# Layer statistics and a flag sent through DRAM instead of TensorE, with sums copied by ScalarE and a rewritten schedule

## The chip, the core and the metric

One NeuronCore of a Trainium2 chip runs the kernel. The metric is the device time of one execution in microseconds (us), taken as the median of several runs. The engines are TensorE (PE in the profile; PEld is its weight load), VectorE (DVE), ScalarE (ACT), GpSimd (POOL) and SyncE (SP). SP only issues transfers here; GpSimd issues those that add to what lies at their destination.

## The reference

The input `x` has 2048 rows of 640 numbers. It is normalized row by row, and the result is the sum of the input, a state-space convolution with a skip term, and a two-layer network with Mish between the layers.

```python
xn = (x - mean(x)) / sqrt(var(x) + 1e-5)            # over the 640 columns
# A: K[d, l] = 2 Re(sum_n C[d, n] exp(A[d, n] dt[d] l));  y = causal convolution of xn with K
a = y + xn * D_skip
# B: w1 is 640 x 1728, w2 is 1728 x 640
h = xn @ w1 + b1
b = (h * tanh(softplus(h))) @ w2
return x + a + b
```

## The kernel before

The rows are cut into four blocks of 512 (`NB`), which the kernel holds transposed: 640 columns as five groups (`KD`) of 128 partitions, 512 rows along the free axis. The 1728 hidden columns are 14 tiles (`NF`), all of 128 but one of 64. Every float32 operand of a product is split into two float16 parts, hi and lo, and a product is made of three matmuls (hi hi, lo hi, hi lo).

For each block and each hidden tile, TensorE makes the first product (`mm1`, L807), ScalarE and VectorE work out Mish in eight steps (L890 to L926), and TensorE adds the tile's second product (`mm2`, L859) to five sums `ACC`, one bank of PSUM each. The second product of a tile comes three tiles after its first (`LAG`). In blocks 1 to 3 twelve of the tiles go in six pairs (`PAIRS`): sums of weights and sums of input quarters replace part of the products (L827), which takes small copies and additions between product groups: `cV`, `cY` on ScalarE (L1049, L1050), `z`, `w` on VectorE (L1053, L1057).

Beside this run:
- the normalization of the next block c. SP loads its rows (L1106), VectorE takes mean and variance (L627 to L629), GpSimd makes `st_row`, 128 partitions by 2 x 4 numbers: four means and four reciprocal deviations (L633, L634, L1213). TensorE transposes them into 8 rows of 128 (`spread`, L638), in the bank `TR` that the pairs also use; ScalarE copies them out of PSUM (`sr`, L642); SP writes them to DRAM (`sd`, L646) and reads them back spread over all 128 partitions, means and deviations (`bc`, L650). VectorE then subtracts and multiplies in each of the five groups of the transposed block `XT` (L654, 2 x 5 steps), after which come the hi and lo parts (L565, L568) and the differences for the pairs (L613 to L620);
- the convolution as two running sums over time with three coefficients per column (`skip_a` to `skip_e`, L743 to L763), which is what it is for small steps and rates. Whether the inputs allow that, and the scaling of the split, is checked on the chip: VectorE leaves one number in each partition (`ok`, L728), a matmul with a matrix of ones adds them over the partitions (`ok_sum`, L731), VectorE compares with 127.5 (L737) and each engine reads the flag (`load_flag`, L734). If it is set, a general version runs behind;
- the output of a finished block: the sums leave PSUM (`join`: k = 0 and 1 on VectorE, L768; 2 to 4 on ScalarE, L770), GpSimd adds the input by an accumulating transfer (L548), adds that to `XT` by another (L773) and stores it (L776). The last block is drained by VectorE and SP (L933, L934).

The first block's normalization and first products, up to 20 us, are a hand-written list (`ORDER`). Behind it the order is a plan made when the program is built (`Plan`): each step has a cost, predecessors, a buffer to take or drop, and for transfers a size. TensorE's steps are in the order in which they are added. From these and the costs each other step gets a due time, worked backwards, and each engine takes the ready step that is due first. The plan sets only the order; on the chip semaphores hold each step until its inputs are there.

Of the kernel before, what the change touches and what calls it, by code (L numbers as in the profile page):

```python
# [20 lines left out]
P = 128  # L21
# [37 lines left out]

class Plan:  # L60


    GAP = {"PE": 0.22, "ACT": 0.12, "DVE": 0.12, "SP": 0.0, "POOL": 0.3}
# [74 lines left out]
    def run(self):  # L138
        self.dues()
        todo = {e: {} for e in self.t}  # L140
# [312 lines left out]
def body(ctx: ExitStack, tc: tile.TileContext, x, xT, logA, Aim, Cr, Ci, logdt, vec, w1, w1T, w2, w2T, out):  # L453
# [29 lines left out]
    ones = cst.tile([P, P], F32, name="ones")  # L483
    g.memset(ones, 1.0)
# [42 lines left out]
    pl.pool("b", [[row.tile([P, TB], F32, name=f"bc{j}") for j in range(2)]])  # L527
# [108 lines left out]
    def spread():  # L636

        pe.transpose(TR[:2 * NT, 0:P], NX["st"].rearrange("p j i -> p (j i)"), ident)  # L638

    def spread_a():  # L640
        NX["sr"] = tmp.tile([2 * NT, P], F32, name="sr")
        a.copy(NX["sr"], TR[:2 * NT, 0:P])  # L642

    def spread_d():
        NX["sd"] = dram.tile([2 * NT, P], F32, name="sd")
        sp.dma_start(NX["sd"], NX["sr"])  # L646

    def spread_l(c):
        for j in range(2):
            sp.dma_start(pl["b", c][j], NX["sd"][j * NT:(j + 1) * NT].rearrange("(o i) p -> o (i p)", o=1).to_broadcast([P, TB]))  # L650

    def norm_t(c, k, j):
        z = XT[c][:, k]
        v.tensor_tensor(z, z, pl["b", c][j], op=(OP.subtract, OP.mult)[j])  # L654
# [9 lines left out]
    def mode_ops():  # L664
# [6 lines left out]
        yield "ACT", 3.4, lambda: a.activation(t()[:, 0], t()[:, 0], AF.Exp)  # L671
# [3 lines left out]
        for k in range(KD):  # L675
            yield "ACT", 0.5, lambda k=k: a.activation(t()[:, 2, k], t()[:, 2, k], AF.Copy, accum_out=sm[:, 0, k:k + 1])
# [53 lines left out]
    def ok_sum():  # L730
        pe.matmul(TR[:, 0:1], ones, SM["ok"], start=True, stop=True)  # L731
# [4 lines left out]
    def ok_end():  # L736
        v.tensor_scalar(flag, TR[0:1, 0:1], P - 0.5, None, op0=OP.is_lt)  # L737
# [27 lines left out]
    def join(b, k):  # L765
        r = pl["r", b, k]
        if k < 2:
            v.tensor_scalar(r, ACC[k], 1 / SO, None, op0=OP.mult)  # L768
        else:
            a.activation(r, ACC[k], AF.Copy, scale=1 / SO)  # L770
# [165 lines left out]
    def whole():  # L936
# [9 lines left out]
        def chain(b, f, pre, drop=()):  # L946
# [3 lines left out]
            if b > 0 and f in PAIRS:  # L950
                add(("sX", *n), A, 0.36, sig, b, f, PX, CA, pre=[("two", *n)], take=("s", ("s", *n), 2))
                add(("vX", *n), V, 0.38, mul, b, f, PX, CA, pre=[("sX", *n)], take=("A", ("A", *n), 1))
                add(("sg", *n), A, 0.36, sig, b, f, PZ, CB, pre=[("three_b", *n), ("sX", *n)])
                add(("v1", *n), V, 0.38, mul, b, f, PZ, CB, pre=[("sg", *n), ("vX", *n)], drop=[("s", *n)])
            else:
                add(("sg", *n), A, t(0.60, 0.36), sig, b, f, pre=pre, take=("s", ("s", *n), 2))
                add(("v1", *n), V, t(0.68, 0.38), mul, b, f, pre=[("sg", *n)], take=("A", ("A", *n), 1), drop=[("s", *n)])
            add(("a1", *n), A, t(0.63, 0.36), mish_a1, b, f, pre=[("sg", *n)], take=("p", ("p", *n), 1), drop=[("s", *n)])
            add(("a2", *n), A, t(0.63, 0.36), mish_a2, b, f, pre=[("a1", *n)])
            add(("a3", *n), A, t(0.63, 0.36), mish_a3, b, f, pre=[("a2", *n)])  # L960
            add(("v3", *n), V, t(0.61, 0.36), mish_v3, b, f, pre=[("a3", *n), ("v1", *n)], drop=[("p", *n)])
            add(("a4", *n), A, t(0.54, 1.44), mish_a4, b, f, pre=[("v3", *n)], take=("h", ("h", *n), 1))
# [40 lines left out]
        for f in range(3, NF):  # L1003
# [4 lines left out]
            if f == 7:  # L1008
                add(("spread", 1), M, 0.1, spread, pre=[("rs", 1)])
# [338 lines left out]
```

## Time and profile before

| | |
|---|---|
| median of 3 runs | 357.88 us (357.68 to 357.89) |
| span of the profiled execution, first to last instruction | 356.0 us |
| granted TensorE clock, mean | 1.000 |
| instructions | 6197 |
| traffic of the transfers | 48.75 MB |

In the profile a group is named by line, engine, operation and `out<-in`, with its count, its busy time and the mean duration of one instruction in ns. Durations overlap a little: an instruction is fed while the one before it finishes, so a step of 0.72 us is followed by the next after 0.61. The chain of waits is followed back from the last instruction; each of its pieces has a start, a length and what ran. In the timeline the columns are start, duration, engine, line and operation, and in brackets the idle time before it and what ended that. A POOL or SP transfer there is its issue, not its movement; the page's last part has the time from issue to landing.

### The profile page before, as it was taken

Reading aid. Unit: us, or ns where it says so; the run is one execution under the profiler, and the core shown is the slowest. Engines: PE = TensorE matmul, PEld = TensorE weight load, DVE = VectorE, ACT = ScalarE, POOL = GpSimd, SP = SyncE. Lnnn points to the kernel's source line nnn. Section 1 sums busy time; section 2 is a strip of 40 time slices with the busy share of each in tenths; the row PEclk is TensorE's granted clock in tenths of the full one; section 3 lists DMA queues with packets and bytes.
Section 4 is the critical chain, followed back from the end, with each engine's and each line's share of the span. In section 5 each row is a group of like instructions: output and inputs, shape, how many; then the busy total and the mean of one; then the engine's idle time right before and its main releaser. Section 6 shows DMA issues by size and latency. Waiting matters only on the chain.

```text
span 356.0 us, 6197 instructions
## 1 busy us (share of the span) xinstructions
PE 350.0 (98%) x2257; PEld 215.1 (60%) x2257; DVE 305.9 (86%) x583; ACT 295.8 (83%) x620; POOL 48.9 (14%) x74
## 2 busy tenths in 40 slices
PE   7999999999999999999999999999999999999996
PEld 6754444444666666665566666566566666666543
DVE  5989989989999999999999877899988878895552
ACT  4699999987598699989899977989989979877650
POOL 2200010000014221000004341000002443000000
PEclk9999999999999999999999999999999999999999
DMA  7869964402819926910445982931000994032004
GB/s 266 327 175 288 321 217 121 142 0 66 287 56 159 295 71 142 347 40 3 130 151 88 252 204 77 309 120 40 28 0 7 164 216 102 18 58 32 2 2 152
DMA packets 26052, 48.75 MB, mean 137 GB/s; under 512 B 3592, under 2 KB 6944, under 8 KB 26016
## 3 DMA queue, kind: packets, MB, share of 16 engines
q1 hardware_dynamic: 19488, 34.86, 30.0%
q0 software_dynamic: 6240, 13.11, 18.5%
q8 instruction: 19, 0.31, 0.4%
q10 hardware_dynamic: 288, 0.33, 0.3%
q14 instruction: 17, 0.14, 0.2%
HBM read 39.10 MB, written 5.26 MB: 125 GB/s over the span
## 4 chain that ended last, share of the span: by engine, by line
PE 96%; DVE 1%; DMA 1%; ACT 0%; issue 0%
PE acc L859 48%; PE h L827 18%; PE h L807 12%; PE tr L827 12%; PE h L800 2%; PE h L789 2%; PE tr L789 1%; DMA x<-in_A_u_dram 1%; PE acc L1236 0%; DVE st L627 0%; DVE st L628 0%; ACT x L1224 0%; PE acc L873 0%; PE acc L871 0%; PE acc L870 0%; DVE w1l L556 0%
## 5 line engine op out<-in xcount | busy, mean ns | idle before, releaser
L859 PE MATMUL acc<-hi,w2h 128*128 128x512 f16 x273 | 100.9, 379 | 0.0
L859 PE MATMUL acc<-hi,w2l 128*128 128x512 f16 (+1 forms) x265 | 99.7, 379 | 0.0
L859 PE MATMUL acc<-lo,w2h 128*128 128x512 f16 x253 | 93.3, 379 | 0.0
L859 PEld LDWEIGHTS <-w2h 128*128 128x128 f16 x526 | 50.9, 98 | 48.3 <-issue 2.1
L890 ACT ACTIVATE s<-h,cv 128x512 f32<-128x512 f32 (+1 forms) x55 | 32.7, 595 | 28.6 <-PE h L827 23.4
L827 PEld LDWEIGHTS <-w1h 128*128 128x128 f16 x432 | 42.3, 98 | 10.7
L910 DVE SCALAR_TENSOR_TENSOR A<-p,A 128x512 f32<-128x512 f32 (+1 forms) x56 | 37.1, 662 | 8.5 <-ACT p L906 8.2
L859 PEld LDWEIGHTS <-w2l 128*128 128x128 f16 x273 | 25.6, 98 | 30.7 <-issue 1.1
L926 DVE SCALAR_TENSOR_TENSOR lo<-A,hi 128x512 f16<-128x512 f32 x52 | 35.5, 683 | 8.0 <-ACT hi L916 8.0
L894 DVE SCALAR_TENSOR_TENSOR A<-h,bs,s 128x512 f32<-128x512 f32 (+1 forms) x55 | 34.9, 637 | 6.2 <-ACT s L890 6.2
L898 ACT ACTIVATE p<-s,kc 128x512 f32<-128x512 f32 (+1 forms) x56 | 39.4, 703 | 0.6
L902 ACT ACTIVATE p<-p,kc 128x512 f32<-128x512 f32 (+1 forms) x56 | 39.4, 703 | 0.5
L906 ACT ACTIVATE p<-p,kc 128x512 f32<-128x512 f32 (+1 forms) x56 | 39.3, 702 | 0.4
L916 ACT ACTIVATE hi<-A 128x512 f16<-128x512 f32 x52 | 32.5, 626 | 2.6 <-DVE A L910 2.5
L548 POOL DMA_DIRECT2D r<-in_xT_dram x15 | 13.4, 1003 | 131.7 <-DVE r L768 66.3
L749 DVE TENSOR_TENSOR_SCAN g<-g,car,kc 128x512 f32<-128x512 f32 x20 | 25.6, 1278 | 1.7 <-ACT g L743 1.7
L827 PEld LDWEIGHTS <-w1l 128*128 128x128 f16 x216 | 21.1, 98 | 8.2
L753 DVE TENSOR_TENSOR_SCAN g<-g,car,g 128x512 f32<-128x512 f32 x20 | 25.5, 1276 | 0.0
L827 PE MATMUL tr<-xh,w1l 128*128 128x256 f16 x90 | 24.5, 273 | 0.0
L827 PE MATMUL tr<-xh,w1h 128*128 128x256 f16 x90 | 24.5, 273 | 0.0
L827 PE MATMUL tr<-xl,w1h 128*128 128x256 f16 x90 | 24.5, 273 | 0.0
L827 PEld LDWEIGHTS <-swh 128*128 128x128 f16 x216 | 21.1, 98 | 4.4
(177 smaller groups left out, 726.6 us busy)
## 6 DMA issues: line engine op xcount, KB each, us to landing
w<-in_w_dram SPq DMA_DIRECT2D x25, 320.0 KB, 4.9
x<-in_A_u_dram SPq DMA_DIRECT2D x14, 320.0 KB, 5.0
w<-in_w2T_dram SPq DMA_DIRECT2D x15, 288.0 KB, 6.4
w<-in_B_w_dram SPq DMA_DIRECT2D x13, 320.0 KB, 3.4
w<-in_w1T_dram SPq DMA_DIRECT2D x13, 320.0 KB, 7.0
xt<-in_xT_dram SPq DMA_DIRECT2D x15, 256.0 KB, 5.6
r<-in_xT_dram POOLq DMA_DIRECT2D x15, 256.0 KB, 5.6
xt<-r POOLq DMA_DIRECT2D x15, 256.0 KB, 4.6
```

The costliest lines, as they stand in the source:

```text
L749: v.tensor_tensor_scan(g1[:, 1:], g1[:, 1:], zero.to_broadcast([P, TB]), car[:, 1, k:k + 1], op0=OP.add, op1=OP.add)
L807: pe.matmul(o, w, x, start=(j == 0), stop=(j == len(order) - 1))
L827: pe.matmul(o, p, q, start=start and n == 1, stop=n == 3 * len(w), skip_group_check=True)
L859: pe.matmul(o, w, x, start=start, stop=stop)
L890: a.activation(pl["s", b, f][:, c], bank(b, f)[:, c] if h is None else h, AF.Sigmoid, bias=cv[:, f:f + 1], scale=1 / SH)
L894: v.scalar_tensor_tensor(pl["A", b, f][:, c], bank(b, f)[:, c] if h is None else h, bs[:, f:f + 1], pl["s", b, f][:, c], op0=OP.add, op1=O ...
L898: a.activation(pl["p", b, f][:, cols(f)], pl["s", b, f][:, cols(f)], AF.Arctan, bias=one, scale=-1.0)
L902: a.activation(p, p, AF.Square, bias=pi4, scale=2.0)
L906: a.activation(p, p, AF.Tanh, bias=mb, scale=MG)
L910: v.scalar_tensor_tensor(A, pl["p", b, f][:, cols(f)], MC, A, op0=OP.add, op1=OP.mult)
L916: a.activation(hi, A, AF.Copy, scale=MA * SA / SH)
L926: v.scalar_tensor_tensor(lo, A, MA * SA / SH, hi, op0=OP.mult, op1=OP.subtract)
```

## The change

- The transposes `spread`, the copies `spread_a` and the matmul `ok_sum` go, with the matrix `ones`. The statistics are written to DRAM from `st_row` as GpSimd leaves it, element by element in transposed order: 8 x 128 numbers of 4 bytes.
- GpSimd stores the mean with its sign changed. Only the deviations are spread into `bc` (one row buffer in place of two). The means are added to `XT` by five accumulating transfers per block, issued by GpSimd, whose source is the row in DRAM repeated for 128 partitions; VectorE is left with the multiplication.
- The `ok` numbers go to DRAM and back as one row of 128; VectorE takes their minimum and compares it with 0.5.
- ScalarE makes all five copies of the sums of a block.
- In the plan, the costs of most steps and two of the gaps are changed, the orders that follow from `spread`, `sr` and `ok_sum` go, and a table `SHIFT` moves the due times of 139 numbered steps by -30 to +30 us.

```diff
+SHIFT = [e.split(":") for e in (
+    "5:16 27:12 30:-15 33:19 36:-20 51:-17.5 55:7.5 61:5 67:-4.5 72:-6.5 79:4 83:-9.5 84:-6.5 90:-16 97:-30 105:7.5 "
...
-    GAP = {"PE": 0.22, "ACT": 0.12, "DVE": 0.12, "SP": 0.0, "POOL": 0.3}
+    GAP = {"PE": 0.17, "ACT": 0.14, "DVE": 0.12, "SP": 0.0, "POOL": 0.3}
...
+        ops = list(self.ops.values())
+        for i, x in SHIFT:
+            for u in ("due", "soft"):
+                ops[int(i)][u] += float(x)
...
-    pl.pool("b", [[row.tile([P, TB], F32, name=f"bc{j}") for j in range(2)]])
+    pl.pool("b", tiles(row, "bc", 1, [P, TB]))
...
-    def spread():
-        pe.transpose(TR[:2 * NT, 0:P], NX["st"].rearrange("p j i -> p (j i)"), ident)
-    def spread_a():
-        NX["sr"] = tmp.tile([2 * NT, P], F32, name="sr")
-        a.copy(NX["sr"], TR[:2 * NT, 0:P])
     def spread_d():
         NX["sd"] = dram.tile([2 * NT, P], F32, name="sd")
-        sp.dma_start(NX["sd"], NX["sr"])
+        sp.dma_start(NX["sd"].rearrange("r p -> p r"), NX["st"].rearrange("p j i -> p (j i)"))
     def spread_l(c):
-        for j in range(2):
-            sp.dma_start(pl["b", c][j], NX["sd"][j * NT:(j + 1) * NT].rearrange("(o i) p -> o (i p)", o=1).to_broadcast([P, TB]))
-    def norm_t(c, k, j):
+        sp.dma_start(pl["b", c], NX["sd"][NT:2 * NT].rearrange("(o i) p -> o (i p)", o=1).to_broadcast([P, TB]))
+    def center(c, k):
+        g.dma_start(XT[c][:, k], NX["sd"][0:NT].rearrange("(o i) p -> o (i p)", o=1).to_broadcast([P, TB]), accum_op=OP.add)
+    def norm_t(c, k):
         z = XT[c][:, k]
-        v.tensor_tensor(z, z, pl["b", c][j], op=(OP.subtract, OP.mult)[j])
+        v.tensor_tensor(z, z, pl["b", c], op=OP.mult)
...
-    def ok_sum():
-        pe.matmul(TR[:, 0:1], ones, SM["ok"], start=True, stop=True)
+    def ok_row():
+        NX["ok"] = tmp.tile([1, P], F32, name="ok_row")
+        z = dram.tile([P], F32, name="ok_dram", bufs=1)
+        sp.dma_start(z.rearrange("(p o) -> p o", o=1), SM["ok"])
+        NX["okd"] = z
+    def ok_back():
+        sp.dma_start(NX["ok"], NX["okd"].rearrange("(o p) -> o p", o=1))
     def ok_end():
-        v.tensor_scalar(flag, TR[0:1, 0:1], P - 0.5, None, op0=OP.is_lt)
+        z = tmp.tile([1, 1], F32, name="ok_all")
+        yield lambda: v.tensor_reduce(z, NX["ok"], axis=AX.X, op=OP.min)
+        yield lambda: v.tensor_scalar(flag, z, 0.5, None, op0=OP.is_lt)
...
     def join(b, k):
         r = pl["r", b, k]
-        if k < 2:
-            v.tensor_scalar(r, ACC[k], 1 / SO, None, op0=OP.mult)
-        else:
-            a.activation(r, ACC[k], AF.Copy, scale=1 / SO)
+        a.activation(r, ACC[k], AF.Copy, scale=1 / SO)
...
-                add(("cV", *n), A, 0.36, lambda: a.copy(PVS, PV), pre=[("one", *n)] + ([] if first else [("w", *p0)]))
-                add(("cY", *n), A, 0.36, lambda: a.copy(PY, PX), pre=[("cV", *n), lastC])
+                add(("cV", *n), A, 0.27, lambda: a.copy(PVS, PV), pre=[("one", *n)] + ([] if first else [("w", *p0)]))
+                add(("cY", *n), A, 0.304, lambda: a.copy(PY, PX), pre=[("cV", *n), lastC])
...
-            add(("sr", c), A, 0.25, spread_a, pre=[("spread", c)])
-            add(("sd", c), S, 0.1, spread_d, pre=[("sr", c)], kb=4.0)
+            add(("sd", c), S, 0.1, spread_d, pre=[("rs", c)], kb=200.0)
...
-                add(("n", c, k, 0), V, 0.62, norm_t, c, k, 0, pre=[("lxt", c), ("bc", c)], drop=[("b", c)])
-                add(("n", c, k, 1), V, 0.62, norm_t, c, k, 1, pre=[("n", c, k, 0)], drop=[("b", c)])
+                add(("n", c, k, 0), G, 1.0, center, c, k, pre=[("lxt", c), ("sd", c)], kb=512.0)
+                add(("n", c, k, 1), V, 0.602, norm_t, c, k, pre=[("n", c, k, 0), ("bc", c)], drop=[("b", c)])
...
+        add(("okd",), S, 0.1, ok_row, pre=last, kb=1.0)
+        add(("okr",), S, 0.1, ok_back, pre=[("okd",)], kb=1.0)
+        fns = list(ok_end())
+        add(("oke", 0), V, 0.2, fns[0], pre=[("okr",)])
+        add(("oke",), V, 0.17, fns[1], pre=[("oke", 0)])
...
-        g.tensor_copy(NX["st"][:, 0], NX["mv"][:, :, 0])
+        g.tensor_scalar(NX["st"][:, 0], NX["mv"][:, :, 0], -1.0, None, op0=OP.mult)
```

More of the change, by code (lines that the diff above doesn't have):

```diff
@@ L958, in chain @@
[L958 to L962, printed above, removed]
@@ L1138, in whole @@
             for j in range(4):
[L1139 removed]
+                add(("ss", i, j), V, 0.336, sum_w, i, j, pre=both + ([("ss", i - 1, 3)] if i and j == 0 else []) + ([("ss", i, 0)] if j == 1 else [("ss", i, 1), ("ss", i, 2)] if j == 3 else []),
                     take=("t", ("ss", i, j // 2), 3 if j == 0 else 1) if j in (0, 2) else None, drop=drops[j])
```

84 lines of the change are left out of this document (38 added, 46 removed), and 9 rows, old and new, of the table SHIFT.

## The prediction

> **What bounds the kernel now.** I read the page first (busy time of each engine, the forty slices, the chain that ended last), then the waits of TensorE, then the chain of waits piece by piece, and last the stretches in which the changed operations run.
>
> ```profile
> PE 350.0 (98%) x2257; PEld 215.1 (60%) x2257; DVE 305.9 (86%) x583; ACT 295.8 (83%) x620; POOL 48.9 (14%) x74
> PEclk9999999999999999999999999999999999999999
> PE 96%; DVE 1%; DMA 1%; ACT 0%; issue 0%
> PE tr L1246 <- POOL ident masks.py:199: 1.5, 1, 1.5
> PE acc L1236 <- ACT x L1224: 1.0, 1, 1.0
> ```
>
> The first three lines are the page's: TensorE (PE) is busy 98%, its granted clock is full in all slices, and it carries 96% of the chain. Busy time alone wouldn't settle it, since modelled matmul ends overlap the gaps. The last two lines are all that the view of TensorE's waits holds, and both belong to the opening (L1246 fills time with idle products, L1236 transposes the first input). So I followed the chain, whose columns are start, length and what ran:
>
> ```profile
> 9.18 0.34 DVE xl L1242
> ...
> 20.34 3.24 PE h L807 x15
> ...
> 46.24 3.24 PE h L807 x15
> 49.48 0.11 PE tr L638
> 49.58 3.24 PE acc L859 x15
> ...
> 134.91 0.11 PE tr L638
> ...
> 219.51 0.11 PE tr L638
> ...
> 321.59 0.12 PE tr L731 x2
> 321.71 1.32 PE acc L859 x6
> ...
> 324.01 1.29 PE acc L859 x6
> ...
> 352.60 0.02 issue
> ```
>
> Each piece begins where the one before it ends. 15 matmuls of 512 columns take 3.24 us in the early and the late pieces, 0.216 us each, and no piece between 20.34 and 352.60 belongs to another engine. For 332 us TensorE waits for nothing. Whatever frees VectorE, ScalarE or a queue in that stretch saves nothing; the program gets shorter only by TensorE instructions that go away, or at its two ends.
>
> **What goes from TensorE.** Three transposes of the statistics (L638) and the flag's matmul (L731, in two passes). On the chain they are 0.11 + 0.11 + 0.11 + 0.12 = 0.45 us, and the six products behind L731 take 1.32 in place of 1.29, so 0.48 us in all. Nothing hides them: the pieces on either side touch. When they go the next matmul group moves up, if what it needs is there.
>
> **The ends.** At the start the chain runs over the load of the input, VectorE and ScalarE until 9.5, where TensorE's piece begins; the hand-written opening is kept, and the memset of `ones` that goes lies on GpSimd (POOL) outside this chain. At the end the last store and its drain stay. I take zero for both, with bounds of plus and minus 0.3 us: the order of everything else moves, so a shift of the size of the opening's last VectorE step (0.34 us, the first row of the fence above) can't be excluded either way.
>
> **VectorE and ScalarE.**
>
> ```profile
> L654 DVE TENSOR_TENSOR xt<-xt,bc 128x512 f32<-128x512 f32 x30 | 20.0, 683 | 0.0
> L768 DVE TENSOR_SCALAR r<-acc 128x512 f32<-128x512 f32 x6 | 4.0, 683 | 0.0
> L770 ACT ACTIVATE r<-acc 128x512 f32<-128x512 f32 x9 | 5.2, 594 | 1.2 <-PE acc L859 0.8
> L642 ACT COPY sr<-tr 8x128 f32<-8x128 f32 x3 | 0.7, 238 | 0.0
> 226.00:262.00 36.00, 36.00 (x232) 22.18 (x231) 34.20 (x57) 33.14 (x73) 0.00 (x0) 1.00 0.30 104
> ```
>
> The 15 subtractions leave VectorE (half of the first row, 15 x 0.683 = 10.2 us), and so do the six copies of sums (4.1 us): 14.3 of 305.9. ScalarE takes those copies over, 6 x 0.594 = 3.6 us, and loses the three copies of `sr`, 0.7: it gains 2.9. On the path to the end both count zero. The relief is real where it falls: in the last row, the stretch ahead of the fourth block, VectorE is busy 34.2 of 36.0 us, and five subtractions, 3.4 us, leave it.
>
> The copies have a deadline. At a block boundary the five sums must be copied out before TensorE writes the next block's first products over them:
>
> ```profile
> 188.28 0.68 DVE L768 TENSOR_SCALAR r<-acc 128x512 f32<-128x512 f32 x1
> 189.78 0.68 DVE L768 TENSOR_SCALAR r<-acc 128x512 f32<-128x512 f32 x1
> 192.00 0.38 PE L859 MATMUL acc<-hi,w2h 128*128 128x512 f16 x1
> ```
>
> The second copy ends at 189.78 + 0.68 = 190.46, TensorE needs the first bank at 192.00: over 1.5 us to spare. From 188.28 to 192.00 ScalarE has 3.7 us for two copies of 0.594 that it did not have; 2.5 are left for the Mish steps and sigmoids, which are wanted three tiles later. It fits if the planner puts the copies first. I take zero; the upper bound is one lost copy pair, 1.2 us, at each of three boundaries.
>
> **The statistics.** Today they wait for a place on TensorE and in its bank; after the change the rows go to DRAM as GpSimd leaves them. The third time is the tightest:
>
> ```profile
> 212.11 0.18 POOL L1213 COPY st_row<-mv 128x4 f32<-128x4 f32 x1
> 220.06 0.91 POOL L773 DMA_DIRECT2D xt<-r  x1 [5.96 <-DVE xt L763]
> 224.02 0.56 POOL L776 DMA_DIRECT2D out_dram<-xt  x1 [3.04 <-DMA xt<-r]
> 231.46 1.29 DVE L654 TENSOR_TENSOR xt<-xt,bc 128x512 f32<-128x512 f32 x2
> 258.21 1.31 PE tr L827 x12
> SPq L650 <- DMA sd<-sr: 4.3, 3, 3.0
> xt<-r POOLq DMA_DIRECT2D x15, 256.0 KB, 4.6
> r<-in_xT_dram POOLq DMA_DIRECT2D x15, 256.0 KB, 5.6
> L548 POOL DMA_DIRECT2D r<-in_xT_dram x15 | 13.4, 1003 | 131.7 <-DVE r L768 66.3
> q1 hardware_dynamic: 19488, 34.86, 30.0%
> ```
>
> The rows are ready at 212.3. The small write of them was waited for up to 3.0 us on SP's queue; the new one has 1,024 elements of 4 bytes. Below, I price it like the old one. Above: the last row gives 0.30 x 16 x 356 / 19488 = 0.088 us a packet of some 2 KB, and if each element cost as much, 64 on each of 16 engines add 5.6 us. So it lands between 215.3 and 220.9. Then GpSimd issues five accumulating transfers, at 1.003 us each, which land 4.6 to 5.6 us after issue: the last one at 225 to 231.5. VectorE began its subtractions at 231.46 today and no longer does them. So even the slow end is in time and the step costs zero; I take the fast end, being nearest the row of the same write. The first two blocks' statistics come in the same order. GpSimd's added issue time is 15 x 1.003 = 15.0 us on an engine that is 14% busy; behind it in its queue stand the output's accumulations and stores, none of which TensorE waits for soon. On SP the row broadcast halves (three transfers fewer), and what stands behind its wait are weight-check loads.
>
> A rule of the Trainium skill speaks against this write: "DMA: Bandwidth & Descriptors", Rules for kernel authors, says that a strided last dimension becomes one descriptor per element and should be rearranged to be contiguous. By that page's 10.5 ns a packet (section Bandwidth), 64 per engine would be an estimated 0.7 us; no run here shows a 4-byte write of data. By it the sum would stay as it is.
>
> **The flag.**
>
> ```profile
> L728 DVE TENSOR_TENSOR ok<-ok,z x1: 153/153/153, 314.2 to 314.2; 128x1 f32<-128x1 f32 x1
> L734 PEldq TENSOR_LOAD <-flag x1: 487/487/487, 330.7 to 330.7; - x1
> ```
>
> From 314.4 it now takes two transfers, up to 3.0 us each by the row above, and two small VectorE steps of 0.15: ready near 320.7, and TensorE reads it at 330.7, ten microseconds later. Cost zero; without that cover, up to 6 us.
>
> **The sum.** 356.0 - 0.48 = 355.5 us of span. The runs' median is 357.88, 1.9 above the profiled span (launch and end, outside it; I keep it): **357.4 us**, 0.13% less. A measurement of this kernel can tell about 0.2%, 0.7 us, from no change, so the likeliest answer is "within".
>
> **Due times and planned costs.** They reorder ScalarE, VectorE, SP and GpSimd; TensorE's own order is written out and stays. As TensorE waits for none of them now, there is no wait to remove, so the gain is zero; what it may cost is the first rival.
>
> **The rivals.**
> - *New due times misplace ScalarE's copies inside the pairs (slower).* Each pair's second product group waits for two short copies:
>
> ```profile
> 157.41 0.37 ACT L1049 COPY pvs<-tr 128x256 f32<-128x256 f32 x1 [0.52 <-PE tr L827]
> 157.68 0.38 ACT L1050 COPY h<-tr 128x256 f32<-128x256 f32 x1
> 158.67 0.98 PE tr L827 x9
> ```
>
>  The copies end at 158.06, TensorE goes on at 158.67: 0.6 us, the tightest place that I found. Against it: today's order keeps it everywhere. For it: the planned costs of ScalarE's steps are cut, so the plan holds less reserve, and over a hundred due times move by up to 30 us. It decides once two steps of about 0.6 us stand ahead of the copies: 0.6 us of stall. At three such pairs, one in each later block, 1.8: 359.2 us. Chance 0.12.
> - *The five copies at the boundaries come too late (slower).* From the point where more than 2.5 us of other ScalarE work goes ahead; up to 1.2 us at three boundaries: 361.0, half of it 359.2. Chance 0.06.
> - *The accumulating transfers queue on GpSimd behind two stores that wait for their data (slower).* Each store costs the wait for the accumulation before it, 4.6 to land and 0.9 of issue: 11 us behind 225 to 231.5, so VectorE would begin at 236 to 242.5 in place of 231.46, with 3.4 us less to do, and end its preparation 1 to 8 us later than today. It decides once that exceeds the lead that the preparation has on the products at 258.21; with half of it passed on once, 4.5 us, 361.9. Chance 0.05.
> - *The gain is eaten by short waits (no change).* The 0.48 us come back as tenths in 18 pairs: 357.5 to 358.5. Nothing in the trace shows such waits now. Chance 0.17.
> - *Faster by over 0.2%.* It needs another 0.24 us beyond all of TensorE's removed work, from the ends; 357.1 with my 0.3. Chance 0.08.
>
> **How the numbers follow.** The forecast has 0.52, with no change 0.69 within; slower 0.12 + 0.06 + 0.05 = 0.23; faster 0.08. The range runs from 357.0 (0.48 and the 0.3 at the ends, rounded) to 359.4, which holds the pairs' and half of the boundaries' case; left out are the queue's case, worse stalls and little below, about 0.15.
>
> **What would show it.** Right: no L638 or L731 pieces, a chain of touching TensorE pieces from 20.3 to about 352.1, no new line in the waits of TensorE, 15 multiplications and no copy of sums on VectorE. Wrong: a wait of TensorE on ScalarE's copies inside a pair (first rival), on sums at 107, 192 or 276 (second), on hi/lo parts of the input near 174 or 258 (third), or a TensorE piece that begins before 9.5.

## The result and the profile after

The changed kernel takes **381.78 us** (median of five runs, 380.98 to 385.35), the kernel before 357.89 beside it. The ratio is 1.069, 95% interval 1.0657 to 1.0726: 23.9 us slower. The profiled execution of it took 385.35 us, with a span of 382.3. Where some executions of a run came out over 1.5% slower than its others (two of x3's four, one of x4's four), the time given is the median of the others.

The page of the changed kernel (TensorE's busy time, its granted clock in forty slices, the chain that ended last):

```profile
PE 357.0 (93%) x2252; PEld 216.9 (57%) x2252; DVE 294.6 (77%) x563; ACT 296.9 (78%) x623; POOL 62.5 (16%) x88
PEclk9999999999999999959999999989999999999999
PE 53%; DMA 21%; DVE 16%; ACT 5%; issue 3%; POOL 1%; SPq 0%; POOLq 0%
```

TensorE has five instructions less (2252 in place of 2257) and VectorE's busy time is 11.3 us shorter; 14.3 were foreseen. But TensorE is busy for 93% of the span in place of 98%, transfers (DMA) now carry 21% of the chain, and in one slice the granted clock is half. The span is 26.3 us longer: TensorE is idle 25.3 us in place of 6.0, and busy 7.0 us longer with five instructions less. Pieces of the chain, with start, length and what ran:

```profile
147.93 8.61 DMA w<-in_w1T_dram
156.58 7.71 DMA xt<-sd
164.31 0.69 DVE xt L666
...
166.57 4.00 PE h L844 x18
...
222.77 8.72 DMA sd<-st_row
231.55 3.90 DMA bc<-sd
235.71 8.27 DMA xt<-sd
244.00 0.69 DVE xt L666
...
337.86 6.74 DMA ok_dram<-ok
344.65 3.24 DMA ok_row<-ok_dram
```

Where the chain of before was TensorE without a gap, it is now, at the three places shown, transfers, then VectorE, then TensorE. (It leaves TensorE between 35 and 111 us as well, but there TensorE itself waited little, 5.3 us in the 100 from 40 on.) In order: a load of weights and an accumulating transfer that takes off a mean; the statistics' small write, the broadcast and another accumulating transfer; the flag's write and read. The load of weights and the broadcast stand in the chain because the profile names what landed last; nothing in the code makes an accumulating transfer wait for either. In both cases an older transfer of GpSimd's own landed at the same moment (at 156.3 the first accumulating one of the block, at 235.4 one of the output's), and that is the likelier releaser. VectorE at the first of these places, as its timeline shows (start, length, line, operation; in brackets its idle time before it and what ended that):

```profile
149.24 0.68 DVE L927 SCALAR_TENSOR_TENSOR A<-p,A 128x512 f32<-128x512 f32 x1
156.29 0.69 DVE L666 TENSOR_TENSOR xt<-xt,bc 128x512 f32<-128x512 f32 x1 [6.37 <-DMA xt<-sd]
158.49 0.69 DVE L666 TENSOR_TENSOR xt<-xt,bc 128x512 f32<-128x512 f32 x1 [1.51 <-DMA xt<-sd]
164.31 0.69 DVE L666 TENSOR_TENSOR xt<-xt,bc 128x512 f32<-128x512 f32 x1 [1.96 <-DMA xt<-sd]
166.11 0.41 DVE L1064 TENSOR_TENSOR h<-h,pvs 128x256 f32<-128x256 f32 x1
```

The multiplications (L666) prepare the next block's input, but they stand at the head of VectorE's queue, and VectorE takes its instructions in order. Behind them stands the sum L1064 of the block under way, which TensorE needs at once. TensorE's waits have such entries in place of none:

```profile
PE tr L844 <- ACT h L1061: 4.7, 3, 2.6
PE acc L876 <- DVE lo L943: 3.8, 3, 3.0
PE h L844 <- DVE h L1064: 3.5, 1, 3.5
PE h L817 <- DVE A L911: 2.7, 1, 2.7
```

(Total, times, longest, in us.) Why the transfers are late shows in two views. GpSimd's timeline at block 1:

```profile
48.16 0.65 POOL L1223 TENSOR_SCALAR st_row<-mv 128x4 f32<-128x4 f32 x1
59.77 2.92 POOL L662 DMA_DIRECT2D xt<-sd  x3 [10.96 <-DMA sd<-st_row]
68.81 0.90 POOL L662 DMA_DIRECT2D xt<-sd  x1 [6.12 <-issue]
70.99 0.88 POOL L662 DMA_DIRECT2D xt<-sd  x1 [1.27 <-issue]
```

The rows are ready at 48.8, the small write lands 11 us later, three accumulating transfers are issued, and the fourth only when the first has landed. And the stretches of time (start and end, length, busy time and count for PE, PEld, DVE, ACT and POOL, granted clock, DMA share, GB/s), the first two at block 1's statistics, the third at block 2's, the others at block 3's:

```profile
49.50:59.30 9.80, 9.37 (x65) 4.80 (x64) 9.62 (x21) 9.77 (x21) 0.00 (x0) 1.00 0.79 30
59.50:64.00 4.50, 4.50 (x23) 2.06 (x21) 2.06 (x6) 2.27 (x6) 2.92 (x3) 1.00 0.89 276
138.20:146.50 8.30, 8.30 (x69) 5.53 (x69) 8.09 (x16) 7.83 (x17) 0.51 (x1) 1.00 0.14 32
223.20:231.30 8.10, 8.10 (x59) 5.52 (x58) 6.25 (x9) 5.84 (x14) 2.20 (x4) 1.00 0.68 82
231.50:240.00 8.50, 7.92 (x53) 5.08 (x52) 5.26 (x9) 5.94 (x16) 3.59 (x5) 1.00 0.98 267
```

While block 1's small write is under way the DMA engines count as 79% busy and move 30 GB/s; as soon as it has landed, 276. There the write of 4 KB is not only slow, what is issued behind it comes late as well. Four weight loads stood on SP's queue just behind it. The view of the changed kernel's load line L561, for those issued from 49.3 to 51.3, closes with their time from issue to landing:

```profile
DMA to landing us min/median/max: 12.4/12.8/13.1
```

The same view of the kernel before, of the three such loads (L543) issued from 48.7 to 51.3:

```profile
DMA to landing us min/median/max: 3.2/3.3/3.4
```

Outside SP's queue too: the output store that GpSimd issued at 222.70 landed at 231.50, in the moment in which the small write issued at 222.77 did. Block 2, where TensorE loses most, is another case: no load was issued behind the small write (the DMA share is 0.14), because SP, which takes its instructions in order too, stood at the broadcast's read until the write had landed (its wait 7.9 us), 8.4 us after the write's issue. Six weight loads and the first three accumulating transfers then started within 6 us of one another.

### The profile page after: what moved, and what is told of

Same layout as the page of the kernel before. It is cut to its first block, busy times and chain, and to the rows that moved or that the text cites. A ratio compares the mean times of both kernels' runs of the same rounds, so it can differ in the third digit from the quotient of the medians.

```text
span 382.3 us, 6201 instructions
## 1 busy us (share of the span) xinstructions
PE 357.0 (93%) x2252; PEld 216.9 (57%) x2252; DVE 294.6 (77%) x563; ACT 296.9 (78%) x623; POOL 62.5 (16%) x88
## 4 chain that ended last, share of the span: by engine, by line
PE 53%; DMA 21%; DVE 16%; ACT 5%; issue 3%; POOL 1%; SPq 0%; POOLq 0%
PE acc L876 25%; PE h L844 13%; PE tr L844 7%; DMA w<-in_B_w_dram 7%; DMA xt<-sd 6%; PE h L824 3%; DMA sd<-st_row 2%; DMA w<-in_w1T_dram 2%; DVE A L911 2%; DMA ok_dram<-ok 2%; PE h L806 2%; DVE g L773 1%; DVE lo L943 1%; DVE A L927 1%; ACT s L907 1%
## 5 line engine op out<-in xcount | busy, mean ns | idle before, releaser
L876 PE MATMUL acc<-lo,w2h 128*128 128x512 f16 x253 | 94.3, 383 | 3.8 <-DVE lo L943 3.8
L844 PEld LDWEIGHTS <-w1l 128*128 128x128 f16 x216 | 21.2, 98 | 15.6 <-issue 7.9
```

Source lines behind the costliest of these rows:

```text
L844: pe.matmul(o, p, q, start=start and n == 1, stop=n == 3 * len(w), skip_group_check=True)
L876: pe.matmul(o, w, x, start=start, stop=stop)
```

## The experiments

The theory that I took into the first runs, "late statistics": the small write and the accumulating transfers land far later than the order of the work assumes, and VectorE's multiplications wait for them with TensorE's work behind. The rivals: "copies and flag" (ScalarE's copies or the flag's two transfers), and "due times" (the table `SHIFT` orders the work badly). The recorded expectations call the accumulating transfer that takes off a mean a center, and the copies of the sums joins.

**One part at a time (four runs).** *x1*, the kernel before with ScalarE's copies and the flag through DRAM:

```diff
-        pe.matmul(TR[:, 0:1], ones, SM["ok"], start=True, stop=True)
...
+        sp.dma_start(z.rearrange("(p o) -> p o", o=1), SM["ok"])
...
+        sp.dma_start(NX["ok"], NX["okd"].rearrange("(o p) -> o p", o=1))
...
-        v.tensor_scalar(flag, TR[0:1, 0:1], P - 0.5, None, op0=OP.is_lt)
...
+        yield lambda: v.tensor_reduce(z, NX["ok"], axis=AX.X, op=OP.min)
+        yield lambda: v.tensor_scalar(flag, z, 0.5, None, op0=OP.is_lt)
...
-        if k < 2:
-            v.tensor_scalar(r, ACC[k], 1 / SO, None, op0=OP.mult)
-        else:
-            a.activation(r, ACC[k], AF.Copy, scale=1 / SO)
+        a.activation(r, ACC[k], AF.Copy, scale=1 / SO)
```

> The kernel before with two parts of the change alone: ScalarE copies all sums, and the flag goes through DRAM; costs, gaps and due times are those of before. Theory 'late statistics' (the element-wise write and the accumulating broadcasts land far later than the plan assumes, and VectorE's multiplications wait for them at the head of its queue): these parts cost almost nothing, 357.0 to 359.5 us, no new wait of TensorE over 1 us. Rival 'copies and flag': they carry the loss, above 368 us, with TensorE waiting at 107, 192 and 276 us and for the flag's readers.

*x2*, the changed kernel with `SHIFT = []`:

> The changed kernel with the table of shifted due times empty, all else kept. Theory 'late statistics': the loss stays, 372 to 388 us, with VectorE waiting 10 us or more in all for the accumulating transfers. Rival 'due times': the order was spoilt by the table, so 357.4 to 362 us without it.

*x3*, as x2, and VectorE subtracts the means from a broadcast tile again (L662 goes, two steps at L666); the small write stays:

> The changed kernel without the table, and with the means subtracted by VectorE from a second broadcast row as before; the element-wise write stays. Theory 'late statistics': with the accumulating transfers gone the last group is ready some 15 us sooner, about half of the loss or more goes, 359 to 370 us; the element-wise write still takes 8 us or more. If the write alone were the cause: 375 to 385. Rival 'due times': like the kernel without the table.

*x4*, as x2, and TensorE transposes the statistics again, which then go to DRAM in whole rows; the accumulating transfers stay:

> The changed kernel without the table, and with the statistics transposed by TensorE, copied by ScalarE and written in whole rows as before; the accumulating transfers stay. Theory 'late statistics': the write is 6 us shorter but starts later for its place on TensorE, and the accumulations keep their 17 to 21 us, so 365 to 382 us. If the element-wise write alone were the cause: 358 to 361.

Measured: x1 363.92 us (ratio 1.018, 1.0155 to 1.0204), x2 397.35 (1.1139, 1.1062 to 1.1217), x3 384.6 (two executions, no interval; 388.15 is the median of all four), x4 368.63 (1.0329, 1.0287 to 1.0371). The rival "due times" falls: without the table it is 15.6 us worse. Of x2's loss most goes with the small write (x4, 28.7 us less), some with the accumulating transfers (x3, 12.8 less). x2 and x3 came out above the ranges that the theory gave them, x3 where I had put the small write alone. And x1 missed its range too. VectorE's timeline of x1:

```profile
314.98 0.42 DVE L913 SCALAR_TENSOR_TENSOR A<-p,A 128x256 f32<-128x256 f32 x1
322.21 0.27 DVE L742 TENSOR_REDUCE ok_all<-ok_row 1x1 f32<-1x128 f32 x1 [6.82 <-DMA ok_row<-ok_dram]
322.52 0.14 DVE L743 TENSOR_SCALAR flag<-ok_all 1x1 int32<-1x1 f32 x1
322.60 0.43 DVE L1054 TENSOR_TENSOR h<-h,pvs 128x256 f32<-128x256 f32 x1
```

The flag's write, 128 numbers of 4 bytes, took 9.4 us to land. The flag itself isn't needed until later, but VectorE's minimum waits for it at the head of the queue, 6.8 us, with L1054 behind, and TensorE waited 3.3 us for that. The same pattern a second time, in a part that I had held to be free.

**The disputed cost by itself, and an order that knows it (four runs).** *z1*, the kernel before with eight small writes on SP's queue, each followed by a read that waits for it (a transfer's landing is then the next issue):

> The kernel before, with eight small writes put on SP's queue one after the other in the stretch from about 302 us on, each followed by a read of 512 bytes of what it wrote, so that each lands alone. The arithmetic is unchanged. Theory 'late statistics': the writes of single elements to DRAM are slow by themselves: 128 elements of 4 bytes (the flag's write) land 6 to 9.5 us after issue, 1024 elements of 4 bytes in transposed order (the statistics' write) 7 to 12 us, while 8 whole rows of 512 bytes and one row of 512 bytes land within 3.5 us, and 128 rows of 512 bytes within 5. The same 128 elements written into one row of SBUF tell whether DRAM or the piece's size sets it: over 6 us if the size does, under 4 if DRAM does. Rival 'contention': the 8 to 12 us seen come from the bulk loads around the statistics; then in this quieter stretch all eight land within 4 us of their issue. Time as the kernel before, 357 to 360 us, by both.

SP's timeline of z1 (L1207 is the read):

```profile
248.36 0.38 SPq L1210 DMA_DIRECT2D pb_dram<-st_row  x1
257.06 0.24 SPq L1207 DMA_DIRECT2D sr<-pb_dram  x1
259.17 0.38 SPq L1211 DMA_DIRECT2D pb_dram<-st_row  x1
270.71 0.23 SPq L1207 DMA_DIRECT2D sr<-pb_dram  x1
271.90 0.34 SPq L1212 DMA_DIRECT2D pb_dram<-st_row  x1
273.30 0.23 SPq L1207 DMA_DIRECT2D sr<-pb_dram  x1
...
286.23 0.34 SPq L1215 DMA_DIRECT2D pb_dram<-st_row  x1
289.29 0.21 SPq L1207 DMA_DIRECT2D sr<-pb_dram  x1
...
325.48 0.55 SPq L1217 DMA_DIRECT2D sr<-st_row  x1
328.14 0.22 SPq L1207 DMA_DIRECT2D sr<-pb_dram  x1
```

| write | to landing, us |
|---|---|
| 128 x 4 bytes side by side in DRAM (the flag) | 8.7 |
| 1024 x 4 bytes in transposed order (the statistics) | 11.5 |
| 128 x 32 bytes | 1.4 |
| 8 rows of 512 bytes (as before) | 2.7 |
| 128 rows of 512 bytes | 3.9 |
| 128 x 4 bytes, 512 bytes apart in DRAM | 3.1 |
| one row of 512 bytes | 1.2 |
| 128 x 4 bytes side by side into a row of SBUF | 2.7 |

"Contention" falls: the slowest write ran in a quiet stretch, as the view of stretches has it (259.60 to 270.60):

```profile
259.60:270.60 11.00, 11.00 (x74) 7.09 (x73) 8.87 (x15) 9.40 (x23) 0.00 (x0) 1.00 0.04 0
```

Neither the number of pieces nor their size alone does it: the same 128 numbers of 4 bytes land in 3.1 us 512 bytes apart (and that between transfers that filled the DMA engines), or in 2.7 in SBUF. What is slow, among the shapes tried, is 4-byte pieces written beside one another in DRAM; why, no run shows. The page "DMA: Bandwidth & Descriptors" of the Trainium skill (Specifications) says that below 512 bytes the DMA engines read, modify and write. That could fit slow neighbours, but no run shows it, and being under 512 bytes doesn't make a write slow by itself here: runs of 32 bytes landed in 1.4 us and 4-byte pieces 512 bytes apart in 3.1. z1 ran the writes from 248 us on and took 357.77 us (one execution), like the kernel before: two slow writes with nothing behind them cost nothing.

*y1* is the whole change with an empty table and a planner that is told the measured landings; *y4* the same without the accumulating transfers; *y5* as x2 with the statistics in runs of 16 bytes (so that rows are normalized with the statistics of others). The main lines:

```diff
+LAT = {'sd': 12.0, 'nc': 9.0, 'bc': 6.6, 'okd': 9.4, 'okr': 4.0, 'jx': 5.6, 'fa': 5.2, 'fs': 5.6}   # y1
+LAT = {'sd': 12.0, 'bc': 6.6, 'okd': 9.4, 'okr': 4.0}                                              # y4
...
-        sp.dma_start(NX["sd"].rearrange("r p -> p r"), NX["st"].rearrange("p j i -> p (j i)"))
+        sp.dma_start(NX["sd"].rearrange("(j a) (b i) -> (a b) j i", j=2, i=NT), NX["st"])          # y5
```

> The whole change, with the table of shifted due times empty and the planner told other durations: 12 us for the statistics to land, 9 for a center, 6.6 for the broadcast of the inverse deviations, 9.4 and 4 for the flag's two transfers, 5.2 to 5.6 for the accumulating transfers and stores of the last layer, and no more than three transfers of GpSimd under way. Theory 'late statistics': the loss is the order, written for transfers that land far sooner; the work that hides them exists once they are planned as long as they are. Then 357.4 to 363 us, and TensorE's waits on VectorE's z and A fall from 15 us and more to under 4. Rival 'no cover': there is too little other work ready between the statistics and the multiplications, whatever the order; then TensorE still waits on VectorE or ScalarE for over 8 us and the time is 368 to 390 us.

> The change with the table of shifted due times empty and the means subtracted by VectorE from a broadcast tile (as in the run with VectorE's subtractions), and the planner told 12 us for the statistics, 6.6 for the broadcast, 9.4 and 4 for the flag's transfers. Theory 'late statistics': the same kernel untold took 388.15 us; told, VectorE's queue is no longer headed by a multiplication whose statistics are 10 us out, so 357.4 to 363 us. Rival 'no cover': 375 to 390 us, as untold.

> The change with the table of shifted due times empty, and the statistics written as 256 runs of 16 bytes in place of 1024 single elements; the statistics then stand in other rows of the table in DRAM, so that rows are normalized with the statistics of others. All else as in the run with the empty table (397.35 us, statistics landing 9.8 to 11.8 us after issue). If the number of pieces sets the landing, it falls to 4 to 6 us and the time to 375 to 388 us. If being under some size is enough to make it slow, the landing stays at 8 to 12 us and the time at 390 to 402.

Measured: y1 379.42 us (1.0585, 1.0567 to 1.0604), y4 377.55 (1.0535, 1.0518 to 1.0553), y5 372.40 (1.0382, 1.0346 to 1.0417), statistics landing after 2.7 to 4.5 us. So the shape decides the landing, and y5 gained more than I had put on it. But my theory of y1 and y4 fell: planned as late as the statistics are, the kernels are still some 20 us slower. What they waited for instead is in y4's timeline of ScalarE, 8.4 us on a weight load:

```profile
152.67 0.74 ACT L708 ACTIVATE w<-w 128x640 f32<-128x640 f32 x1 [8.45 <-DMA w<-in_w1T_dram]
```

That load was issued on SP at 139.2, right behind the small write (138.78 to 149.28). The view of stretches of y1 at the same place:

```profile
139.00:151.00 12.00, 12.00 (x95) 7.61 (x93) 9.33 (x14) 7.60 (x17) 0.98 (x2) 1.00 0.73 21
151.80:157.60 5.80, 0.38 (x3) 0.10 (x2) 2.87 (x5) 4.47 (x13) 0.58 (x1) 0.92 0.99 320
157.60:163.00 5.40, 5.40 (x21) 3.01 (x21) 3.33 (x7) 4.10 (x11) 2.70 (x3) 0.50 1.05 336
```

12 us at 21 GB/s, then 320. A planner that is told when the statistics land still doesn't know that everything issued beside them lands late too. The theory became: beside its own lateness, the write makes the other transfers late. No run takes that alone away (a slow write with loads on either side, and nobody waiting for it); it rests on these stretches and landings. The write does not fill the DMA engines by itself, since alone in z1 it left their share at 0.04; what slows the others no run shows.

**The writes in another shape (four runs).** *w1* is x1 with the flag's numbers 512 bytes apart; *w3* the whole change with its own table, flag apart and statistics in runs of 16 bytes (again with the rows' statistics exchanged, as in y5); *w5* the same with twice the memory for GpSimd's descriptors; *w4* the whole change with the flag apart and the statistics first moved column by column into 8 rows of SBUF. The main lines:

```diff
-        z = dram.tile([P], F32, name="ok_dram", bufs=1)
-        sp.dma_start(z.rearrange("(p o) -> p o", o=1), SM["ok"])
+        z = dram.tile([P, P], F32, name="ok_dram", bufs=1)          # w1, w3, w5, w4
+        sp.dma_start(z[:, 0:1], SM["ok"])
...
-_BACC = {"dynamic_dma_scratch_size": 1024}
+_BACC = {"dynamic_dma_scratch_size": 2048}                          # w5
...
+        for r in range(2 * NT):                                     # w4
+            sp.dma_start(z[r:r + 1], st[:, r:r + 1])
+        sp.dma_start(NX["sd"], z)
```

> The kernel before with ScalarE's joins and the flag through DRAM (363.92 us with the flag's 128 elements side by side, landing 9.35 us after issue), now with the flag's 128 elements written 512 bytes apart and read back from there. Theory 'neighbours': elements of 4 bytes are slow only where they are written beside one another in DRAM, as the probe showed (8.7 us side by side, 3.1 us 512 bytes apart); the write lands in 3 to 4 us, TensorE's wait on VectorE's h near 319 is gone, and the time is 357.3 to 359 us. Rival 'joins': what was lost came from the copies that ScalarE took over; then 361 to 365 us.

> The whole change with its own table of due times, and two writes given another shape in DRAM: the flag's elements 512 bytes apart, the statistics in runs of 16 bytes (the rows are then normalized with statistics of others). The order of all work is that of the changed kernel. Theory 'neighbours': the plan was right but for these two writes and for GpSimd's transfers, of which three are under way at a time; statistics land in 2.5 to 4.5 us, the flag in 3 to 4, and 381.78 falls to 358 to 366 us, what is left being waits on the multiplications after the late centers. Rival 'plan': the order suits the chip badly for other reasons too; then over 368 us.

> As the run with both fast writes (the whole change, its own due times, flag 512 bytes apart, statistics in runs of 16 bytes), and the memory for GpSimd's descriptors 2048 bytes in place of 1024. Theory: the fourth center is issued only when the first has landed because that memory is full; with twice as much all five are issued within 5 us of one another, the last lands 8 to 12 us after the first is issued in place of 14 to 16, and the time is 1 to 6 us under the other run, 357.3 to 361. Rival: the depth is the queue's own; landings and time as in the other run, within 1 us.

> The whole change with its own due times; the flag's elements 512 bytes apart; the statistics written column by column into 8 rows of SBUF (8 transfers of 128 elements of 4 bytes), then as 8 whole rows to DRAM, so that no TensorE work comes back and all values are the reference's. By the probe's 2.7 us for such a column and 2.7 for 8 rows, with 8 issues of 0.35 us between, the statistics land 5 to 8 us after the first issue. Theory 'neighbours': 358 to 370 us, between the run with both fast writes and halfway to the changed kernel. Rival: writes of single elements are slow anywhere once there are 1024 of them; they land after 9 us or more and the time is 372 to 382.

Measured: w1 358.36 us (1.001, 1.0000 to 1.0019), w3 363.10 (1.0151, 1.0127 to 1.0174), w5 361.79 (1.0107, 1.0090 to 1.0123), w4 375.43 (1.0476, 1.0430 to 1.0522). w1: the copies cost nothing that can be told from noise, x1's loss was the flag's shape. w3 is the result of the study: the order of the changed kernel, two transfers with other addresses, 18.7 of 23.9 us gone. Behind the opening, TensorE's waits of w3 hold one entry over 1 us:

```profile
PE h L844 <- DVE h L1064: 2.1, 1, 2.1
```

Its list of transfers (KB each, median us from issue to landing):

```profile
xt<-sd POOLq DMA_DIRECT2D x15, 256.0 KB, 7.6
sd<-st_row SPq DMA_DIRECT2D x3, 4.0 KB, 3.4
ok_dram<-ok SPq DMA_DIRECT2D x1, 0.5 KB, 1.4
```

Against the changed kernel's 9.7 and 6.7 us, the two writes land after 3.4 and 1.4.

GpSimd's timeline of w5 at block 1: all five accumulating transfers are issued without a pause, so the limit of three was that memory.

```profile
51.47 4.71 POOL L662 DMA_DIRECT2D xt<-sd  x5 [4.44 <-DMA sd<-st_row]
```

but at block 1 the last of them landed at 67.1 as in w3 (67.3): with five under way each took longer (median 9.7 us in place of 7.2). The later blocks gained 2 and 4 us in landing and the kernel 1.3. w4 missed: the statistics took 7.7 to 8.8 us from the first issue to the end, eight issues of 0.64 us with the weight loads behind them, and the time came out in the rival's range without the rival's cause (each column landed 2.0 to 3.8 us after its issue). It bears on the theory all the same. At block 1 the DMA share was 0.27 during these writes, and the four weight loads behind them landed 3.1 to 4.4 us after issue in place of 12.4 to 13.1; yet w4 is 12.3 us slower than w3, which differs from it in the statistics' write alone. So late statistics, with the loads issued some 5 us later behind them, cost about as much in this order without a held-up transfer as the slow write does (14.2, below). How its cost divides between its own lateness and that of the others is open.

**The shares (four runs).** Runs of 16 bytes can stand in the right places if, for the statistics alone, a partition loads four neighbouring rows: `x[0].rearrange("(b p i) d -> b i p d")` in place of `"(b i p) d"`. *v1* is the whole change with this, the flag apart and 2048 bytes; *v2* with the statistics' write alone; *v3* the kernel before without transposes and flag product; *v4* is v3 with accumulating transfers and 2048 bytes.

> The whole change, its own due times, all values the reference's: for the statistics, each partition now loads four neighbouring rows of a chunk, so that its runs of 16 bytes stand in the right places of the table in DRAM; the flag's elements stand 512 bytes apart; GpSimd's descriptor memory is 2048 bytes. By the theory of the slow neighbouring writes it does as the run with wrong rows did, 361 to 362.5 us (361.79). If the statistics' loads suffer from their new order (320 KB in rows of 2560 bytes that are four rows apart), over 364 us.

> The changed kernel with its own due times, and the statistics' write alone made fast (four neighbouring rows on each partition, runs of 16 bytes); the flag's write and the descriptor memory as in the changed kernel. With both writes fast it took 363.10 us. If the statistics' write carried nearly all, 363 to 365 us; my estimate is 365 to 369, because the flag's wait alone cost 5.6 us where the rest stood as before (363.92 against 358.36); over 370 if the flag carries the larger share.

> The kernel before with its own costs and due times, without the three transposes of the statistics and their copies on ScalarE (statistics in runs of 16 bytes straight to DRAM, four neighbouring rows on each partition) and without the flag's product (flag through DRAM, elements 512 bytes apart). VectorE subtracts the means and copies the first two sums, as before. TensorE has 0.48 us less work, so 357.4 to 358.0 us by the theory that only late transfers cost; 359 or more if the order, which the planner now makes otherwise, has waits of its own (its plan has 3.7 us of them).

> As the kernel before without transposes and flag product, but the means taken off by accumulating transfers on GpSimd's queue (descriptor memory 2048 bytes). If these transfers cost nothing once the statistics are early, within 1 us of that run; if their 8 to 11 us to landing come too late for VectorE's multiplications, 2 to 8 us more, 360 to 366, with waits of VectorE at the head of its queue on the accumulated tile.

Measured: v1 362.58 us (1.0129, 1.0114 to 1.0145); v2 367.62 (1.0273, 1.0253 to 1.0293); v3 359.64 (1.0039, 1.0026 to 1.0053); v4 365.18 (1.0204, 1.0163 to 1.0245). v1 is 0.1 us above the theory's range. v3 came out in the range of an order with waits of its own, though its trace has one behind the opening, of 0.3 us. Taken away in this order, the statistics' write carries 14.2 of the 23.9 us (381.78 to v2's 367.62), the flag's 4.5 (to w3's 363.10), the descriptor memory about 1, and some 4 are left: in w5 three short waits of TensorE on VectorE and ScalarE (1.0, 0.6 and 0.4) and about 1 outside the span, of which more below. The flag's share holds for fast statistics: behind its minimum TensorE waited 2.4 us in v2, with half the clock after it, and 1.3 in the changed kernel. It also holds the new order of the statistics' loads, which w3 doesn't have (0.8 us between w5 and v1). v4 against v3: with the order of before, the accumulating transfers cost 5.5 us.

**Is anything left that isn't lateness (two runs)?** *u1* (no accumulating transfers) and *u2* (with them): both writes fast, the planner told the landings, a table of due times searched on the planner's own model.

> The change without the accumulating transfers (VectorE subtracts the means from a broadcast tile), both writes in the fast shape (runs of 16 bytes from four neighbouring rows on each partition; flag 512 bytes apart), ScalarE's copies as in the change. The planner is told 4.8 us for the statistics, 5.8 for the broadcast, 3.8 and 3.2 for the flag, and has a table of shifted due times, searched on its own model against waits at costs 2% higher. TensorE has 0.48 us less work than in the kernel before. If only lateness cost, 357.2 to 358.3 us, the same as before or 0.1 to 0.2% better; if the order on chip has waits that the model does not see, 358.5 to 361.

> The whole change with the accumulating transfers, both writes in the fast shape, GpSimd's descriptor memory 2048 bytes, the planner told 4.8 us for the statistics, 12 for a center, 6.2 for the broadcast, 3.8 and 3.2 for the flag, and a table of shifted due times searched as for its sister run. With the change's own table the same writes took 362.58 us. If the accumulating transfers only need to be planned as long as they are, 357.2 to 359.5; if they cost by crowding GpSimd's queue and the channels, 360 to 365.

Measured: u1 360.03 us (1.0071, 1.0056 to 1.0087), u2 367.19 (1.0266, 1.0252 to 1.0280). Neither beats the kernel before; u1 lies in the range of waits that the model does not see, u2 above both of its ranges. TensorE's waits of u2:

```profile
PE h L836 <- ACT xh L1279: 5.3, 1, 5.3
PE h L847 <- DVE A L941: 0.3, 1, 0.3
```

The first is in the opening, at 8.1: in the order that came of the search, a split of weights whose load had not landed stands ahead on ScalarE (5.2 us at the head of its queue). The granted clock was then 0.71 in the six us from 14 on. That is u2's loss, and the order's fault. Behind it TensorE waits 0.3 us in all: planned as 12 us long, the accumulating transfers make it wait no more. So the 5.5 us of v4 seem to belong to its order and not to the transfers themselves; u2, slower for its opening, doesn't show it in a time. u1 has no long wait either (TensorE ends at 353.20, in place of 352.59), and is 2.1 us slower: 0.9 in the span (356.9), 0.8 outside it, and its profiled run was 0.4 under its median. Four kernels that keep TensorE's transposes (x1, x4, z1, w1) took 1.77 to 1.84 us more than their span in the profiled execution; the fifteen without them, the changed kernel among them, 2.45 to 3.17. What that microsecond is, no run tells; of x2 and x4, which differ only in the statistics' way to DRAM, x2 has it.

## Why the prediction was wrong

- **What goes from TensorE** held: five instructions less, and in w3, with the changed kernel's own order, no wait of TensorE behind the opening is over 2.1 us. That the 0.48 us come off the time no run shows: v3 and u1, without this work and with fast writes, are 1.5 and 2.1 us slower than the kernel before.
- **The copies of the sums** held: w1, copies and all, is within 0.2% of before. The sign of my first rival did appear: in the changed kernel TensorE waited 4.7 us in all for a copy inside a pair (L1061). At 155.76 that copy was late because the step ahead of it on ScalarE had stood 2.8 us waiting for a late weight load; in w3, in the same order, the entry is gone.
- **The statistics: the step that failed.** I priced the small write at 3.0 to 8.6 us and took the fast end as "nearest the row of the same write". It was not the same write: it landed after 8.4 to 10.6 us, 11.5 in z1. The upper bound, from one row's time a packet, was nearer, and short at two of the three times; but the conclusion "even the slow end is in time and the step costs zero" was wrong for three reasons. I asked only when VectorE used to begin, not what stands behind the waiting multiplication in VectorE's queue. I looked at the third time alone, and the second, at block 2, lost most (TensorE idle 8.5 us of the 33 from 140 on, 3.8 of the 41 from 212 on). And I took nothing for the transfers behind it: at block 1 weight loads issued beside it landed after 12.4 to 13.1 us in place of 3.3, and at block 2 SP issued none until it had landed. In the same order with the two writes in another shape (w3), 18.7 of the 23.9 us are gone. The rule of the Trainium skill that I cited ("DMA: Bandwidth & Descriptors", Rules for kernel authors) spoke against the write rightly; the 0.7 us that I estimated from that page's packet time stand against a landing of 8.4 to 10.6.
- **The accumulating transfers** land 8.3 us after issue (median), not 4.6 to 5.6, and three at a time: the last one lands 17 us after the small write at block 1. My third rival had GpSimd's queue as the bottleneck, but put it behind two stores, not in its descriptor memory and beside the loads.
- **The flag**: I had it ready near 320.7, read by TensorE ten microseconds later, at a cost of zero. The cover was real for TensorE's read of the flag, and beside the point: VectorE's minimum waits in order. It cost 4.5 us with the statistics' write fast (v2 to w3) and 5.6 in x1, near the "up to 6 us" that I gave if the cover were gone.
- **The due times**: "no wait to remove, so the gain is zero" was reckoned against the kernel before. In the changed kernel, full of waits, the table is worth 15.6 us (x2).
- **The ends**: the 1.9 us around the span that I kept grew by about 1.

## What to carry to other kernels

A step that leaves the critical engine isn't free because its result is wanted late: look up what stands behind the instruction that waits for it, on every in-order queue, and which transfers are issued behind it. Reckon for a write to DRAM of 4-byte pieces side by side 7 to 12 us, as measured here, and look at what else is issued in that time; give every piece 16 bytes or more, or space them out (512 bytes here), before touching the schedule. When a plan believes that nothing waits and the chip waits, compare each transfer's planned landing with the measured one first.

## What the runs showed that I had not expected

- Beside one 4 KB write the other transfers hardly moved: 21 and 30 GB/s for 10 to 12 us, then 320 and 276 (y1, the changed kernel). The same write alone left the DMA share at 0.04 (z1).
- 32 bytes in place of 4 a piece takes the write of the same 4 KB from 11.5 us to 1.4.
- After waits of TensorE its granted clock was half for some 3 to 10 us: in y1, where it was busy 0.38 us of 5.80, 0.51 in the 6.8 us from 156.8 on; in the changed kernel 0.50 in the 10.2 us from 162.1 on, and the 18 products that elsewhere take 1.97 us took 4.00 at 166.57. A late transfer is paid for twice. "TensorE: Matmul & The Clock Gate" of the Trainium skill (Part 1) puts the loss of clock at one idle window of about 3.4 us. The runs don't settle on such a length of wait: one of 3.3 us in x1 left the clock full in all slices, one of 2.4 us in v2 was followed by 0.57 in the next 3.4 us.
